# Transposing keys and probabilities on VectorE with a block diagonal query, and splitting the last load, in a one-core decode kernel

## The chip, the cores and the metric

The kernel runs on one core of a Trainium2 chip. The metric is the device time of one execution in microseconds (us). All times below are of undisturbed ("fast") runs; the runs of the two kernels compared agree within 0.5 us. A profiled execution also gives a span, from the first to the last instruction, which is about 1.8 us shorter than the time. Times inside a profile count from the start of that span.

## The reference, cut to what matters

One token (x of 1024 elements) is decoded. Part A is attention over a cache of 65,536 keys and values, with 32 query heads in 4 groups of 8 that share keys and values, each of 128 dimensions. Part B is a gated MLP. A gate mixes both.

```python
q = (x @ wq)                                   # 1024 x 4096
scores = einsum('bhqd,bhkd->bhqk', q, k) * Dh ** (-0.5)
p = softmax(scores)
o = einsum('bhqk,bhkd->bhqd', p, v)
a = o.reshape(...) @ wo                        # 4096 x 1024
z = gelu(x @ w_in)                             # 1024 x 3584
b = (z1 * (w_sp * layernorm(z2) + b_sp)) @ w_out
out = g * a + (1 - g) * b                      # g = sigmoid(sum(x * gate_w))
```

In bf16 the cache and the weights are 162 MB, all read once. There is little arithmetic per byte.

## The kernel before

All large inputs come through one ring of five slots, about 4 MB each, loaded by one queue in a fixed order: wq, then keys with w_in and w_out in between, then pairs of key units and value units in turn, at last wo. A load into a slot is issued when the slot's old content has been used. A unit is 8192 keys (or values) of one group, 2 MB.

The key path before: TensorE transposes 128x128 blocks of fp32 (each fp32 is two bf16 features), VectorE and ScalarE copy them from PSUM, and 32-row matmuls make the scores.

```python
def k_piece(n, j):                       # four of these for a unit
    sl, key = use(("k", n))
    for b in (2 * j, 2 * j + 1):
        def tr(e, b=b, pb=pb):
            for t in range(4):
                ins = e.transpose(pf(pb)[:, 128 * t:128 * (t + 1)],
                                  sl[:, 128 * (4 * b + t):128 * (4 * b + t + 1)], idf)
            return ins
        P("PE", tr, r=["idf", key], w=[B(pb)])
        if b in (2, 5, 7):
            P("ACT", lambda e, ...: e.activation(ktb(i), pbf(pb), ACTF.Copy), ...)
        else:
            P("DVE", lambda e, ...: e.tensor_copy(ktb(i), pbf(pb)), ...)
    # ... cut: s_piece() multiplies with the padded query, 8 matmuls for half a unit
```

The ring, and the end of the kernel:

```python
def done(key):                           # frees the slot of a load, issues the next load into it
    n = place[key][0]
    if key == stream[n][0][-1]:
        issue(n + NS + 1)
# ... cut
for i in range(4):                       # wo in four loads of 2 MB; 32 matmuls for each
    sl, key = use(("wo", i))
    # ... cut: 8 rows c times 4 column groups q, accumulated in one bank
P("DVE", lambda e: e.tensor_tensor(orow[0:97, :], pf(FB)[0:97, 0:QW], brow[0:97, :], ALU.add), ...)
# then the store of the output
```

## Time and profile before

| | before |
|---|---|
| time, median | 390.6 us |
| span of the profile | 389.0 us |
| loaded from HBM | 162.0 MB |
| last load seen as landed | 384.5 us |

The page of the kernel before cuts the span into 40 slices of 9.7 us. Digits are tenths of busy time; PEclk is the clock granted to TensorE, in tenths; DMA is the mean busy share of the 16 DMA engines, and the last row is what they moved.

```profile
...
PE   0000689988997998696888696968686949665423
...
DVE  3000181626756675353645353547453526410110
...
PEclk9999996775999999696989696989896969955685
DMA  8999999999999999999999999999999999999991
GB/s 324 431 431 438 415 397 445 440 432 426 431 426 426 424 426 438 430 431 424 430 431 430 431 426 431 430 431 430 433 431 430 429 430 431 430 431 423 428 414 83
...
```

DMA is busy in every slice but the first and the last, at about 430 GB/s. The other rows have gaps everywhere, so the loads set the pace: 162.4 MB at 431 GB/s are 377 of the 389 us.

The DMA queues of the same page (packets, MB, share of 16 engines' time): q1 brings the loads. q8 and q14 fetch instructions.

```profile
...
q1 hardware_dynamic: 5912, 162.01, 97.3%
q8 instruction: 21, 0.34, 0.4%
...
q14 instruction: 4, 0.03, 0.0%
...
```

The chain that ended last, by engine, and the costliest groups (busy us, mean ns of one, then the idle time ahead of them and what ended it):

```profile
...
DMA 62%; PE 33%; DVE 3%; ACT 1%; issue 1%; ACTq 0%; DVEq 0%
...
```

```profile
...
L440 PE MATMUL pb<-arena 128*128 128x128 f32 x1024 | 155.5, 304 | 39.5 <-DMA arena<-in_A_k_cache_dram 38.9
...
L448 DVE COPY arena<-pb 128x1024 bf16<-128x1024 bf16 x160 | 107.4, 687 | 117.1 <-PE pb L440 115.2
L445 ACT ACTIVATE arena<-pb 128x1024 bf16<-128x1024 bf16 x96 | 97.9, 1020 | 162.1 <-PE pb L440 162.1
L510 PE MATMUL pb<-arena 128*32 128x512 bf16 x512 | 39.0, 432 | 15.9 <-DMA arena<-in_A_v_cache_dram 11.7
L464 PE MATMUL pb<-arena 128*32 128x512 bf16 x512 | 45.1, 431 | 3.6 <-ACT arena L445 1.9
...
```

L440 is the key transposes, L448 and L445 their copies, L464 the scores and L510 the product of probabilities and values. The transposes are the largest thing on TensorE, 155.5 us, but the idle time ahead of them ends with a load of keys.

The end, from the timeline in order of time (start, duration, instruction):

```profile
...
374.68 1.04 PE L653 MATMUL pb<-arena 128*1 128x256 bf16 x32 [2.06 <-DMA arena<-in_A_wo_dram]
...
384.54 1.88 PE L653 MATMUL pb<-arena 128*1 128x256 bf16 x32 [3.08 <-DMA arena<-in_A_wo_dram]
386.47 0.43 DVE L659 TENSOR_TENSOR arena<-pb,arena 97x256 bf16<-97x256 f32 x1 [14.06 <-PE pb L653]
386.92 0.63 SPq L662 DMA_DIRECT2D out_dram<-arena  x1
```

The last quarter of wo is seen to have landed at 384.54, then come 32 matmuls, one add and the store. The same 32 matmuls took 1.04 us at 374.68, where the granted clock was 1.00, and 1.88 us at 384.54, where it was 0.50. In between TensorE had been idle for 3.86 us, had run the 32 matmuls before them in 1.88 us (379.59, clock 0.50), and had been idle again for 3.08 us.

### The profile page before, as it was taken

Reading aid. Unit: us, or ns where it says so; the run is one execution under the profiler, and the core shown is the slowest. Engines: PE = TensorE matmul, PEld = TensorE weight load, DVE = VectorE, ACT = ScalarE, POOL = GpSimd, SP = SyncE. Lnnn points to the kernel's source line nnn. Section 1 sums busy time; section 2 is a strip of 40 time slices with the busy share of each in tenths; the row PEclk is TensorE's granted clock in tenths of the full one; section 3 lists DMA queues with packets and bytes.
Section 4 is the critical chain, followed back from the end, with each engine's and each line's share of the span. In section 5 each row is a group of like instructions: output and inputs, shape, how many; then the busy total and the mean of one; then the engine's idle time right before and its main releaser. Section 6 shows DMA issues by size and latency. Waiting matters only on the chain.

```text
span 389.0 us, 6080 instructions
## 1 busy us (share of the span) xinstructions
PE 267.3 (69%) x2692; PEld 181.6 (47%) x2692; DVE 159.7 (41%) x354; ACT 124.3 (32%) x171; POOL 1.5 (0%) x8
## 2 busy tenths in 40 slices
PE   0000689988997998696888696968686949665423
PEld 0000269786776665454555454545455536221111
DVE  3000181626756675353645353547453526410110
ACT  1000041423556656161435161615251606231000
POOL 1000000000000000000000000000000000000000
PEclk9999996775999999696989696989896969955685
DMA  8999999999999999999999999999999999999991
GB/s 324 431 431 438 415 397 445 440 432 426 431 426 426 424 426 438 430 431 424 430 431 430 431 426 431 430 431 430 433 431 430 429 430 431 430 431 423 428 414 83
DMA packets 6769, 162.39 MB, mean 418 GB/s; under 512 B 1492, under 2 KB 1496, under 8 KB 1496
## 3 DMA queue, kind: packets, MB, share of 16 engines
q1 hardware_dynamic: 5912, 162.01, 97.3%
q8 instruction: 21, 0.34, 0.4%
q10 hardware_dynamic: 832, 0.00, 0.1%
q14 instruction: 4, 0.03, 0.0%
HBM read 162.01 MB, written 0.00 MB: 417 GB/s over the span
## 4 chain that ended last, share of the span: by engine, by line
DMA 62%; PE 33%; DVE 3%; ACT 1%; issue 1%; ACTq 0%; DVEq 0%
DMA arena<-in_A_k_cache_dram 38%; PE pb L440 18%; DMA arena<-in_gate_w_dram 10%; DMA arena<-in_A_v_cache_dram 8%; DMA arena<-in_A_wo_dram 6%; PE pb L464 5%; PE pb L557 3%; PE pb L510 3%; PE pb L396 1%; DVE arena L448 1%; PE pb L498 1%; ACT arena L445 0%; PE pb L653 0%; PE pb L605 0%; DVE arena L421 0%
## 5 line engine op out<-in xcount | busy, mean ns | idle before, releaser
L440 PE MATMUL pb<-arena 128*128 128x128 f32 x1024 | 155.5, 304 | 39.5 <-DMA arena<-in_A_k_cache_dram 38.9
L440 PEld LDWEIGHTS pb<-arena 128*128 128x128 f32 x1024 | 127.7, 157 | 80.3 <-DMA arena<-in_A_k_cache_dram 42.5
L448 DVE COPY arena<-pb 128x1024 bf16<-128x1024 bf16 x160 | 107.4, 687 | 117.1 <-PE pb L440 115.2
L445 ACT ACTIVATE arena<-pb 128x1024 bf16<-128x1024 bf16 x96 | 97.9, 1020 | 162.1 <-PE pb L440 162.1
L510 PE MATMUL pb<-arena 128*32 128x512 bf16 x512 | 39.0, 432 | 15.9 <-DMA arena<-in_A_v_cache_dram 11.7
L464 PE MATMUL pb<-arena 128*32 128x512 bf16 x512 | 45.1, 431 | 3.6 <-ACT arena L445 1.9
L378 PE MATMUL pb<-arena 128*128 128x1 f32 x2 | 0.6, 363 | 40.8 <-DVE arena L377 40.8
L491 ACT ACTIVATE arena<-arena 128x512 bf16<-128x512 f32 x32 | 22.8, 714 | 15.4 <-PE pb L498 13.5
L510 PEld LDWEIGHTS pb<-arena 128*32 128x32 bf16 x512 | 11.7, 102 | 30.9 <-issue 19.8
L470 DVE TENSOR_SCALAR_CACHE_REDUCE arena<-pb 128x512 f32<-128x512 f32 x32 | 21.9, 686 | 6.4 <-PE pb L464 5.8
L501 DVE COPY arena<-pb 128x512 bf16<-128x512 bf16 x32 | 13.3, 416 | 24.7 <-PE pb L498 24.7
L378 PEld LDWEIGHTS pb<-arena 128*128 128x128 f32 x2 | 0.5, 313 | 40.8 <-DVE arena L377 40.8
L464 PEld LDWEIGHTS pb<-arena 128*32 128x32 bf16 x512 | 8.3, 96 | 16.9 <-issue 8.4
L498 PE MATMUL pb<-arena 128*128 128x128 bf16 x128 | 15.3, 255 | 0.0
L376 DVE TENSOR_TENSOR arena<-arena 128x8 f32<-128x8 bf16 x1 | 0.2, 168 | 36.1 <-DMA arena<-in_gate_w_dram 36.1
L498 PEld LDWEIGHTS pb<-arena 128*128 128x128 bf16 x128 | 11.5, 117 | 5.7 <-issue 4.2
L557 PEld LDWEIGHTS pb<-arena 128*128 128x128 bf16 x224 | 13.7, 159 | 0.0
L557 PE MATMUL pb<-arena 128*128 128x1 bf16 x224 | 13.7, 198 | 0.0
L653 PE MATMUL pb<-arena 128*1 128x256 bf16 x128 | 5.8, 342 | 9.0 <-DMA arena<-in_A_wo_dram 9.0
L380 ACT ACTIVATE arena<-pb 128x1 f32<-128x1 f32 x1 | 0.2, 171 | 37.0 <-PE pb L378 37.0
L653 PEld LDWEIGHTS pb<-arena 128*1 128x1 bf16 x128 | 3.2, 99 | 11.2 <-DMA arena<-in_A_wo_dram 6.5
L659 DVE TENSOR_TENSOR arena<-pb,arena 97x256 bf16<-97x256 f32 x1 | 0.4, 426 | 14.1 <-PE pb L653 14.1
(87 smaller groups left out, 59.8 us busy)
## 6 DMA issues: line engine op xcount, KB each, us to landing
arena<-in_A_k_cache_dram SPq DMA_DIRECT2D x16, 4096.0 KB, 29.9
arena<-in_A_v_cache_dram SPq DMA_DIRECT2D x16, 4096.0 KB, 34.3
arena<-in_A_wq_dram SPq DMA_DIRECT2D x2, 4096.0 KB, 17.2
arena<-in_A_wo_dram SPq DMA_DIRECT2D x4, 2048.0 KB, 30.5
arena<-in_B_w_in_dram SPq DMA_DIRECT2D x2, 3584.0 KB, 27.8
arena<-in_B_w_out_dram SPq DMA_DIRECT2D x1, 3584.0 KB, 20.5
arena<-in_A_x_dram ACTq DMA_DIRECT2D x1, 2.0 KB, 22.3
arena<-in_gate_w_dram ACTq DMA_DIRECT2D x1, 2.0 KB, 39.0
```

Of the source, the lines that this page charges most:

```text
L396: ins = e.matmul(pf(OB)[32 * cg:32 * cg + 2, :], xw[:, 3 * c + 1 - s:3 * c + 3 - s], sl[:, WQ_N * k + 512 * (4 * s + cg):WQ_N * k + 512 * ...
L440: ins = e.transpose(pf(pb)[:, 128 * t:128 * (t + 1)], sl[:, 128 * (4 * b + t):128 * (4 * b + t + 1)], idf)
L445: P("ACT", lambda e, i=i, pb=pb: e.activation(ktb(i), pbf(pb), ACTF.Copy), w=[("kt", i % NKTS), B(pb)])
L448: P("DVE", lambda e, i=i, pb=pb: e.tensor_copy(ktb(i), pbf(pb)), w=[("kt", i % NKTS), B(pb)])
L464: ins = e.matmul(pf(SCB)[32 * cg:32 * (cg + 1), :], qpad[:, v:v + 32], vw(ktb(first + cg), ev, [[2, 512]]), start=(c == 0 and ev == 0), st ...
L470: P("DVE", lambda e: e.tensor_scalar(scs(n), pf(SCB), 0.0, None, op0=ALU.add, op1=ALU.max, accum_out=maxc[:, n:n + 1]), w=[("sc", n % NSC) ...
L491: P("ACT", lambda e: e.activation(psb(n), scs(n), ACTF.Exp, bias=gcol(g, K_NB), scale=SCALE, accum_out=lp[:, n:n + 1]), r=[("sc", n % NSC) ...
L498: ins = e.transpose(pbf(PTB)[:, 128 * xi:128 * (xi + 1)], psb(n)[:, 128 * xi:128 * (xi + 1)], idb)
L501: P("DVE", lambda e: e.tensor_copy(ptsb(n), pbf(PTB)[:, 0:512]), w=[("ptsb", n % 2), B(PTB)])
L510: ins = e.matmul(pf(OB)[32 * cg:32 * (cg + 1), :], ptsb(n)[:, 128 * xi + 32 * cg:128 * xi + 32 * (cg + 1)], vw(sl, 128 * (8 * cg + 2 * xi) ...
L557: ins = e.matmul(pf(MB)[:, z:z + 1], vw(sl, c0, [[FC, 128]]), xT[:, 2 * i + k:2 * i + k + 1], start=(i == 0 and k == 0 and z == 0), stop=( ...
L653: ins = e.matmul(pf(FB)[32 * q:32 * q + 1, 0:QW], ovec[:, 8 * i + c:8 * i + c + 1], sl[:, DO * c + QW * q:DO * c + QW * (q + 1)], start=(i ...
```

## The change

Its intent is to take the key transposes and their copies off TensorE, PSUM and ScalarE. VectorE transposes 32x32 blocks from SBUF to SBUF. After such a transpose, each quarter of the partitions holds 32 feature pairs of the keys of that quarter alone, so one matmul over 128 partitions would add up four different keys. The query is therefore laid out block diagonally: rows of the result belong to (quarter, piece, head), and the weights are zero where the quarters differ. Four matmuls, for the even and odd features of two halves, add up the 128 features. The probabilities are transposed in the same way. The maximum becomes one for each head, which saves a correction later. The last quarter of wo is loaded in three parts, so that fewer matmuls follow the last landing.

```diff
-        for b in (2 * j, 2 * j + 1):
-            P("PE", tr, ...)                       # 4 fp32 transposes of 128x128
-            P("ACT" or "DVE", ... copy of the bank ...)
+        P("DVE", lambda e: e.transpose(ktb(i).bitcast(F32), sl[:, 2048 * j:2048 * (j + 1)].bitcast(F32)),
+          r=[key], w=[("kt", i % NKTS)])
+        def f(e):
+            for fe in range(4):
+                f2, ev = fe // 2, fe % 2
+                o = QP * fe + 24 - 8 * j
+                ins = e.matmul(pf(sb), qpad[g % 2][:, o:o + 128], vw(ktb(i), 64 * f2 + ev, [[128, 16], [2, 32]]),
+                               start=(j == 0 and fe == 0), stop=(j == 3 and fe == 3))
+            return ins
 ... cut: query layout, one maximum per head
     def pt_piece(n):
-        ... 4 TensorE transposes into PSUM, one copy ...
+        P("DVE", lambda e: e.transpose(ptsb(n), psb(n)), r=[("psb", n % 2)], w=[("ptsb", n % 2)])
 ... cut: 16 matmuls for values as before, other order of blocks
-    for i in range(4):
-        load([("wo", i)], [(0, rows(A_wo, i, 8))])
+    WO = [(0, 0, 8), (1, 0, 8), (2, 0, 8), (3, 0, 4), (3, 4, 6), (3, 6, 8)]
+    for i, c0, c1 in WO:
+        load([("wo", i, c0)], [(0, rows(A_wo, i, 8)[:, DO * c0:DO * c1])])
```

More of the change, by code (lines that the diff above doesn't have):

```diff
@@ L168, in bass_gated_mix__gqa_block_cached__mixer_gmlp__decode_kernel @@
     SLOT = 16384
-    NB = TILES // 8
-    NKTS = 7
+    QP = 152
+    NKTS = 3
     NSC = 10
@@ L187, in bass_gated_mix__gqa_block_cached__mixer_gmlp__decode_kernel @@
     for name, n in [
-        ("RING", NS * SLOT), ("KT", NKTS * 1024), ("SC", NSC * 1024), ("PSB", 1024), ("PTSB", 1024),
-        ("QPAD", G * 128), ("IDB", 128), ("IDF", 256), ("BM", 256), ("ONES", 256), ("SEL", 16 * 32),
+        ("RING", NS * SLOT), ("KT", NKTS * 2048), ("SC", NSC * 1024), ("PSB", 1024), ("PTSB", 1024),
+        ("QPAD", 2 * 4 * QP), ("IDB", 128), ("IDF", 256), ("BM", 256), ("ONES", 256), ("SEL", 16 * 32),
         ("M16", 32), ("M8", 16), ("M32", 64), ("MQ", 32), ("OT", 256), ("XT", KC), ("GW", KC), ("WB", 2), ("MAXC", 2 * G * NU), ("LP", 2 * G * NU),
-        ("COLS", 2 * 64), ("DM", 32), ("QT", 32), ("XW", 3 * KC), ("SELE", 256), ("OSC", 512), ("OV", OC), ("Z", 2 * 28), ("Z2", 2 * 28),
+        ("COLS", 2 * 64), ("DM", 32), ("QT", 32), ("QALL", 128), ("XW", 3 * KC), ("OSC", 512), ("OV", OC), ("Z", 2 * 28), ("Z2", 2 * 28),
         ("ZG", 2 * 28), ("ZE", 2 * 28), ("YB", FC), ("BROW", 2 * QW), ("OROW", QW),
@@ L212, in bass_gated_mix__gqa_block_cached__mixer_gmlp__decode_kernel @@
     xT, gw, wb = ab("XT", KC), ab("GW", KC), ab("WB", 2)
-    qpad = ab("QPAD", G * 128)
+    qpad = [ab("QPAD", 4 * QP, 4 * QP * i) for i in range(2)]
+    qall = ab("QALL", 128)
     maxc, lp, colt = af("MAXC", G * NU), af("LP", G * NU), af("COLS", 64)
@@ L224, in gcol @@
         return col(C_G4 + 11 * g + i)
-    (K_M, K_NB, K_MH, K_D, K_W, K_L, K_LW, K_RL, K_F) = range(9)
+    (K_M, K_NB, K_MH, K_L, K_RL, K_F) = range(6)
     def slot(n):
         return ab("RING", SLOT, (n % NS) * SLOT)
-    ktb = lambda i: ab("KT", 1024, (i % NKTS) * 1024)
+    ktb = lambda i: ab("KT", 2048, (i % NKTS) * 2048)
     scs = lambda n: af("SC", 512, (n % NSC) * 512)
@@ L236, in bass_gated_mix__gqa_block_cached__mixer_gmlp__decode_kernel @@
     bank = [nc.alloc_psum_tensor("pb%d" % i, [128, 512], F32) for i in range(8)]
-    KTB = [0, 1, 2, 3]
-    SCB, PTB, OB, MB = 4, 5, 6, 7
+    FB, PTB, OB, MB = 0, 5, 6, 7
+    SCB = [3, 4]
     pf = lambda i: bank[i][:, :]
@@ L252, in bass_gated_mix__gqa_block_cached__mixer_gmlp__decode_kernel @@
     P("POOL", lambda e: e.tensor_copy(idb, idf), r=["idf"], w=["idb"])
-    P("POOL", lambda e: e.memset(qpad, 0.0), w=["qpad"])
+    for i in range(2):
+        P("POOL", lambda e, i=i: e.memset(qpad[i], 0.0), w=[("qpad", i)])
     P("DVE", lambda e: e.memset(ones, 1.0), w=["ones"])
@@ L257, in bass_gated_mix__gqa_block_cached__mixer_gmlp__decode_kernel @@
     P("DVE", lambda e: e.memset(pf(OB), 0.0), w=[B(OB)])
+    P("DVE", lambda e: e.memset(pf(FB), 0.0), w=[B(FB)])
     P("DVE", lambda e: e.memset(xw, 0.0), w=["xw"])
@@ L369, in bass_gated_mix__gqa_block_cached__mixer_gmlp__decode_kernel @@
     P("DVE", lambda e: e.tensor_reduce(mq, vw(idf, 0, [[1, 16], [16, 8]]), AXX, ALU.add), r=["idf"], w=["mq"])
-    for ev in range(2):
-        P("DVE", lambda e, ev=ev: e.tensor_copy(vw(ab("SELE", 128, 128 * ev), 0, [[64, 2], [1, 64]]),
-                                                vw(idb, ev, [[0, 2], [2, 64]])), r=["idb"], w=["sele"])
+    sele = ab("SC", 512, (NSC - 1) * 1024)
+    KSE = ("sc", NSC - 1)
+    for fe in range(4):
+        P("DVE", lambda e, fe=fe: e.tensor_copy(vw(sele, 128 * fe, [[32, 4], [1, 32]]),
+                                                vw(idb, 64 * (fe // 2) + fe % 2, [[0, 4], [2, 32]])),
+          r=["idb"], w=[KSE])
     P("DVE", lambda e: e.tensor_tensor(z2[:, 0:KC], xT, gw, ALU.mult), r=["xT", "gw"], w=["z2"])
@@ L414, in f @@
     def f(e):
-        for ev in range(2):
-            ins = e.matmul(pf(PTB)[:, 32 * ev:32 * (ev + 1)], ab("SELE", 128, 128 * ev), qT, start=True, stop=True)
-        return ins
-    P("PE", f, r=["sele", "qT"], w=[B(PTB)])
-    for g in range(G):
-        for par in range(2):
-            P("DVE", lambda e, g=g, par=par: e.tensor_copy(
-                vw(qpad, 128 * g + 8 * par, [[80, 2], [32, 2], [1, 8]], 64 * par, 64),
-                vw(pf(PTB), 8 * g, [[0, 2], [32, 2], [1, 8]], 64 * par, 64)), r=[B(PTB)], w=["qpad"])
+        for fe in range(4):
+            ins = e.matmul(pf(PTB)[:, 32 * fe:32 * (fe + 1)], sele[:, 128 * fe:128 * (fe + 1)], qT, start=True, stop=True)
@@ L426, in bass_gated_mix__gqa_block_cached__mixer_gmlp__decode_kernel, with q_piece @@
+        return ins
+    P("PE", f, r=[KSE, "qT"], w=[B(PTB)])
+    P("DVE", lambda e: e.tensor_copy(qall, pf(PTB)[:, 0:128]), w=["qall", B(PTB)])
     nbatch = [0]
     pend = []
+    def q_piece(g):
+        for pb in range(4):
+            P("DVE", lambda e, pb=pb: e.tensor_copy(vw(qpad[g % 2], 24 + 32 * pb, [[QP, 4], [1, 8]], 32 * pb, 32),
+                                                    vw(qall, 8 * g, [[32, 4], [1, 8]], 32 * pb, 32)),
+              r=["qall"], w=[("qpad", g % 2)])
     def k_piece(n, j):
+        g, u = KV[n]
+        if u == 0 and j == 0:
+            q_piece(g)
@@ L431, in k_piece @@
         sl, key = use(("k", n))
-        sl = sl.bitcast(F32)
-        for b in (2 * j, 2 * j + 1):
-            i = nbatch[0]
-            nbatch[0] += 1
-            pb = KTB[i % 4]
-            def tr(e, b=b, pb=pb):
-                for t in range(4):
-                    ins = e.transpose(pf(pb)[:, 128 * t:128 * (t + 1)],
-                                      sl[:, 128 * (4 * b + t):128 * (4 * b + t + 1)], idf)
-                return ins
-            P("PE", tr, r=["idf", key], w=[B(pb)])
-            if b in (2, 5, 7):
-                P("ACT", lambda e, i=i, pb=pb: e.activation(ktb(i), pbf(pb), ACTF.Copy),
-                  w=[("kt", i % NKTS), B(pb)])
-            else:
-                P("DVE", lambda e, i=i, pb=pb: e.tensor_copy(ktb(i), pbf(pb)), w=[("kt", i % NKTS), B(pb)])
+        i = nbatch[0]
@@ new lines, in k_piece @@
+        nbatch[0] += 1
+        P("DVE", lambda e: e.transpose(ktb(i).bitcast(F32), sl[:, 2048 * j:2048 * (j + 1)].bitcast(F32)),
+          r=[key], w=[("kt", i % NKTS)])
+        sb = SCB[n % 2]
+        def f(e):
+            for fe in range(4):
+                f2, ev = fe // 2, fe % 2
[3 more added lines that the diff above has]
+            return ins
@@ L449, in k_piece @@
+        P("PE", f, r=[("qpad", g % 2), ("kt", i % NKTS)], w=[B(sb)])
+        if pend:
+            score_piece(pend.pop(0))
         if j == 3:
             done(("k", n))
-        if j % 2 == 1:
-            pend.append((n, j // 2, nbatch[0] - 4))
-    def s_piece():
-        if not pend:
-            return
-        n, c, first = pend.pop(0)
-        g, u = KV[n]
-        def f(e):
-            for ev in range(2):
-                for cg in range(4):
-                    v = 128 * g + 32 * (2 * c + ev)
-                    ins = e.matmul(pf(SCB)[32 * cg:32 * (cg + 1), :], qpad[:, v:v + 32],
-                                   vw(ktb(first + cg), ev, [[2, 512]]), start=(c == 0 and ev == 0),
-                                   stop=(c == 1 and ev == 1), tile_position=(0, 32 * cg), skip_group_check=True)
-            return ins
-        P("PE", f, r=["qpad"] + [("kt", (first + i) % NKTS) for i in range(4)], w=[B(SCB)])
-        if c == 1:
-            P("DVE", lambda e: e.tensor_scalar(scs(n), pf(SCB), 0.0, None, op0=ALU.add, op1=ALU.max,
-                                               accum_out=maxc[:, n:n + 1]), w=[("sc", n % NSC), ("mx", n), B(SCB)])
-            if u == NU - 1:
-                max_piece(g)
@@ L475, in max_piece, with score_piece @@
+            pend.append(n)
+    def score_piece(n):
+        g, u = KV[n]
+        sb = SCB[n % 2]
+        P("DVE", lambda e: e.tensor_scalar(scs(n), pf(sb), 0.0, None, op0=ALU.add, op1=ALU.max,
+                                           accum_out=maxc[:, n:n + 1]), w=[("sc", n % NSC), ("mx", n), B(sb)])
+        if u == NU - 1:
+            max_piece(g)
     def max_piece(g):
@@ L477, in max_piece @@
           r=[("mx", NU * g + u) for u in range(NU)], w=[("m", g)])
-        P("DVE", lambda e: e.tensor_scalar(gcol(g, K_NB), gcol(g, K_M), -SCALE, None, op0=ALU.mult),
-          r=[("m", g)], w=[("nb", g)])
-    def weight_piece(g):
         P("DVE", lambda e: e.tensor_scalar(dm, m16, gcol(g, K_M), None, op0=ALU.mult), r=["m16", ("m", g)], w=["dm"])
@@ L484, in weight_piece @@
         P("DVE", lambda e: e.tensor_reduce(gcol(g, K_MH), pf(MB)[:, 0:16], AXX, ALU.max), w=[("mh", g), B(MB)])
-        P("DVE", lambda e: e.tensor_tensor(gcol(g, K_D), gcol(g, K_M), gcol(g, K_MH), ALU.subtract),
-          r=[("m", g), ("mh", g)], w=[("d", g)])
-        P("ACT", lambda e: e.activation(gcol(g, K_W), gcol(g, K_D), ACTF.Exp, scale=SCALE), r=[("d", g)], w=[("w", g)])
+        P("DVE", lambda e: e.tensor_scalar(gcol(g, K_NB), gcol(g, K_MH), -SCALE, None, op0=ALU.mult),
+          r=[("mh", g)], w=[("nb", g)])
     def exp_piece(n):
@@ L495, in pt_piece @@
     def pt_piece(n):
-        def f(e):
-            for xi in range(4):
-                ins = e.transpose(pbf(PTB)[:, 128 * xi:128 * (xi + 1)], psb(n)[:, 128 * xi:128 * (xi + 1)], idb)
-            return ins
-        P("PE", f, r=["idb", ("psb", n % 2)], w=[B(PTB)])
-        P("DVE", lambda e: e.tensor_copy(ptsb(n), pbf(PTB)[:, 0:512]), w=[("ptsb", n % 2), B(PTB)])
+        P("DVE", lambda e: e.transpose(ptsb(n), psb(n)), r=[("psb", n % 2)], w=[("ptsb", n % 2)])
     def pv_piece(n):
@@ L507, in f @@
         def f(e):
-            for xi in range(4):
-                for cg in range(4):
-                    ins = e.matmul(pf(OB)[32 * cg:32 * (cg + 1), :],
-                                   ptsb(n)[:, 128 * xi + 32 * cg:128 * xi + 32 * (cg + 1)],
-                                   vw(sl, 128 * (8 * cg + 2 * xi), [[4096, 2], [1, 256]]),
-                                   start=(u == 0 and xi == 0), stop=(u == NU - 1 and xi == 3),
-                                   tile_position=(0, 32 * cg), skip_group_check=True)
+            for b in range(16):
+                cg = b % 4
+                ins = e.matmul(pf(OB)[32 * cg:32 * (cg + 1), :], ptsb(n)[:, 32 * b:32 * (b + 1)],
+                               vw(sl, 128 * b, [[2048, 4], [1, 128]]), start=(u == 0 and b < 4),
+                               stop=(u == NU - 1 and b >= 12), tile_position=(0, 32 * cg), skip_group_check=True)
             return ins
@@ L523, in out_piece @@
           r=[("lp", NU * g + u) for u in range(NU)], w=[("l", g)])
-        P("DVE", lambda e: e.tensor_tensor(gcol(g, K_LW), gcol(g, K_L), gcol(g, K_W), ALU.mult),
-          r=[("l", g), ("w", g)], w=[("lw", g)])
-        P("PE", lambda e: e.matmul(pf(MB)[:, 0:1], bm, gcol(g, K_LW), start=True, stop=True),
-          r=["bm", ("lw", g)], w=[B(MB)])
+        P("PE", lambda e: e.matmul(pf(MB)[:, 0:1], bm, gcol(g, K_L), start=True, stop=True),
+          r=["bm", ("l", g)], w=[B(MB)])
         P("DVE", lambda e: e.reciprocal(gcol(g, K_RL), pf(MB)[:, 0:1]), w=[("rl", g), B(MB)])
-        P("DVE", lambda e: e.scalar_tensor_tensor(gcol(g, K_F), gcol(g, K_RL), gcol(g, K_W), col(C_G),
-                                                  op0=ALU.mult, op1=ALU.mult),
-          r=[("rl", g), ("w", g), "g"], w=[("f", g)])
+        P("DVE", lambda e: e.tensor_scalar(gcol(g, K_F), gcol(g, K_RL), col(C_G), None, op0=ALU.mult),
+          r=[("rl", g), "g"], w=[("f", g)])
         P("DVE", lambda e: e.tensor_scalar(osc, pf(OB), gcol(g, K_F), None, op0=ALU.mult),
@@ L625, in bass_gated_mix__gqa_block_cached__mixer_gmlp__decode_kernel @@
         if k is None and pend:
-            s_piece()
+            score_piece(pend.pop(0))
         if v is not None and v not in started:
@@ L630, in bass_gated_mix__gqa_block_cached__mixer_gmlp__decode_kernel @@
             if k is not None:
-                ready = len(pend)
                 k_piece(k, j)
-                s_piece() if ready else None
             if j == 1 and v is not None:
                 pt_piece(v)
-            if j == 2 and nxt is not None and (k is not None or not pend):
+            if j == 2 and nxt is not None:
                 start_exp(nxt)
@@ L639, in bass_gated_mix__gqa_block_cached__mixer_gmlp__decode_kernel, with f @@
                 pv_piece(v)
-        if v is not None and v % NU == 0:
-            weight_piece(v // NU)
         for a in aux:
             (win_piece if a[0] == "win" else wout_piece)(a[1])
-    FB = KTB[0]
-    for i in range(4):
-        sl, key = use(("wo", i))
-        def f(e, i=i, sl=sl):
-            for c in range(8):
+    for i, c0, c1 in WO:
+        sl, key = use(("wo", i, c0))
+        def f(e, i=i, sl=sl, c0=c0, c1=c1):
+            for c in range(c0, c1):
                 for q in range(4):
+                    o = DO * (c - c0) + QW * q
                     ins = e.matmul(pf(FB)[32 * q:32 * q + 1, 0:QW], ovec[:, 8 * i + c:8 * i + c + 1],
-                                   sl[:, DO * c + QW * q:DO * c + QW * (q + 1)],
-                                   start=(i == 0 and c == 0), stop=(i == 3 and c == 7), tile_position=(0, 32 * q),
-                                   skip_group_check=True)
+                                   sl[:, o:o + QW], start=(i == 0 and c == 0), stop=(i == 3 and c == 7),
+                                   tile_position=(0, 32 * q), skip_group_check=True)
             return ins
         P("PE", f, r=[("ovec", i), key], w=[B(FB)])
+        done(("wo", i, c0))
     P("DVE", lambda e: e.tensor_tensor(orow[0:97, :], pf(FB)[0:97, 0:QW], brow[0:97, :], ALU.add),
```

## The prediction

> **What bounds the kernel now.** The loads. The page's row of slices shows DMA busy at 0.9 or more in every slice but the first and last, mostly at 424 to 431 GB/s; queue q1 is busy for 97.3% of the span. 162.4 MB at 431 GB/s is 377 us of a 389.0 us span; the rest is the start and the end. TensorE's 69% (key transposes 155.5 us), VectorE's 41% and ScalarE's 32% lie under the loads. In the chain of waits DMA has 62%; TensorE's part lies in the first 135 us (it starts late, since gate_w lands at 40 us), yet windows there average 428 GB/s: five ring slots of 4 MB hide it.
>
> The end, from the timeline: the last quarter of wo lands at 384.54, then 32 matmuls at half clock (1.9 us), one add (0.43 us), the store (about 2 us). The load rate falls off from 376 to 384, as the DMA engines do not finish together; this stays.
>
> **What the change does.**
> - Removes 1024 fp32 TensorE transposes (155.5 us busy), their 256 evictions (VectorE 107.4 us, ScalarE 97.9 us), 128 transposes of probabilities (15.3 us) and their copies (13.3 us).
> - Adds 128 VectorE transposes of 128x1024 fp32.[...] The trace's 512-column fp32 evictions took 0.69 us[...]. 128 x 1.2 = 155 us, 32 probability transposes of 0.6 us (estimate, 19 us) and the score reductions (22 us): VectorE rises to about 205 us, 53%. ScalarE falls to about 27 us.
> - Scores become 512 full-width matmuls of 512 columns[...]. TensorE falls to roughly 170 to 200 us.
> - Splits the last load, so that 8 matmuls instead of 32 follow the last bytes: 1.9 us becomes 0.5.
>
> **Critical path.** A pair of key units and one of value units take 19.5 us to load. VectorE needs for them 8 x 1.2 + 2 x 0.7 + 2 x 0.6 = 12.2 us: it keeps up. In the key-only stage two units need about 11 us of VectorE and win 6.7 us of TensorE; I find each slot free 7 us or more before the queue would run dry. So the loads stay the limit. Gained: 1.4 us from the split, and 0.3 us as the instruction fetch (0.34 MB) shrinks by about 40%. 390.6 - 1.7 = 388.9 us.
>
> **Predicted: 388.9 us, range 387.3 to 391.3.** Chances: over 2% faster 0.03, within 2% 0.91, slower 0.06.
>
> **What would show it.** Right: DMA share 0.9 or more in all middle slices at about 430 GB/s; VectorE transposes near 1.2 us; more TensorE idle put down to k_cache and v_cache loads; 8 matmuls (0.5 us) between the last landing and the add; last landing within 1 us of 384.5. Wrong: dips of GB/s between 60 and 135 us, or the load queue waiting on transposes or score matmuls.
>
> **What would make it wrong.** [...]VectorE becomes the limit and the time goes to 392 to 400.[...]

Five passages of this text are cut, since no trace or run of this case shows what they rest on: two on how the 1.2 us for a key transpose was arrived at; the time of the score matmuls; the condition for VectorE to become the limit (key transposes at about twice the cost); and a sum for TensorE at half clock. TensorE's 170 to 200 us contains a term, 110 us for the score matmuls. The 1.2 and 0.6 us for VectorE's transposes, and with them 155, 19, 205, 12.2 and 11 us, were my estimates, which no trace showed at that time; the changed kernel's shows 1.216 and 0.679 us.

## The result, and the profile after

The changed kernel takes 387.72 us (387.70 to 387.94) against 390.62 us: 2.9 us less. The ratio is 0.9926, with a 95% interval of 0.9909 to 0.9943. It is the mean time of one kernel's fast runs over that of the other's in the same rounds, so it is not quite the ratio of the medians.

The slices of the changed kernel, 9.6 us each:

```profile
...
PE   0000668983886888472688383827883929543354
...
DVE  4000078335999997574597574735984748511010
...
PEclk9999969695899999696789697956697978866555
DMA  8999999999999999999999999999999999999994
GB/s 326 435 435 442 374 442 426 429 436 433 435 408 419 435 435 430 428 435 427 431 431 435 433 435 431 435 423 429 435 431 426 428 432 435 430 431 428 419 419 190
...
```

The load rate has hardly changed (420 GB/s in the mean of the span, 418 before). VectorE is now the busiest engine in slices 11 to 15 (96 to 145 us), and TensorE has more gaps. The span is 385.9 us (389.0 before).

Its queues:

```profile
...
q1 hardware_dynamic: 6200, 162.01, 98.1%
q8 instruction: 12, 0.20, 0.2%
...
q14 instruction: 4, 0.03, 0.0%
...
```

The loads are the same 162.01 MB. The instruction fetches of q8 have gone from 21 packets to 12, because 1150 matmuls with their weight loads are gone (2692 became 1542; with 1128 put back as padding, below, the fetches are 21 again).

Its chain by engine, and its groups:

```profile
...
DMA 53%; PE 22%; DVE 22%; issue 1%; ACT 0%; ACTq 0%; DVEq 0%
...
```

```profile
...
L457 PE MATMUL pb<-arena 128*128 128x512 bf16 x512 | 154.4, 442 | 78.5 <-DVE arena L449 76.2
L449 DVE STREAM_TRANSPOSE arena<-arena 128x1024 f32<-128x1024 f32 x128 | 151.3, 1216 | 56.7 <-DMA arena<-in_A_k_cache_dram 50.5
...
L487 ACT ACTIVATE arena<-arena 128x512 bf16<-128x512 f32 x32 | 23.0, 720 | 208.5 <-DVE arena L492 155.3
L492 DVE STREAM_TRANSPOSE arena<-arena 128x512 bf16<-128x512 bf16 x32 | 21.7, 679 | 18.3 <-PE pb L501 18.3
L470 DVE TENSOR_SCALAR_CACHE_REDUCE arena<-pb 128x512 f32<-128x512 f32 x32 | 21.7, 678 | 5.7 <-PE pb L457 5.5
...
```

L449 is the new key transpose: 1216 ns for 1024 fp32 elements per partition. L492 transposes the probabilities, L457 makes the scores, and L487 is the exponential that was there before. The rest of ScalarE's work is gone.

Its end:

```profile
...
382.76 0.60 PE L635 MATMUL pb<-arena 128*1 128x256 bf16 x8 [0.65 <-DMA arena<-in_A_wo_dram]
383.41 0.42 DVE L641 TENSOR_TENSOR arena<-pb,arena 97x256 bf16<-97x256 f32 x1 [13.41 <-PE pb L635]
383.86 0.62 SPq L644 DMA_DIRECT2D out_dram<-arena  x1
```

The last landing is at 382.76 instead of 384.54, and 8 matmuls follow it instead of 32. So the traces show two gains: the loads end 1.7 to 1.8 us earlier, and the tail behind them is 1.3 us shorter (the last matmuls take 0.60 us instead of 1.88). The prediction had the second and only 0.3 us of the first.

To see why the loads end earlier, one more record of the trace is needed. In the trace every large load has 16 semaphore increments at different times, and the kernel goes on at the last of them: for the last load of the kernel before they come from 379.13 to 384.41 us, and the matmuls start at 384.54. The page counts 16 DMA engines; I read each increment as one of them being done with its part. The records do not name the engine, so "engine" below stands for this reading. The table, worked out from these increments, gives for some loads of the kernel before the first landing (us) and how much later each of the sixteen came, in order:

```
load   first   the sixteen, us after the first
  4    51.16   0.00 0.11 0.12 0.15 0.16 0.18 0.20 0.21 0.22 0.27 0.28 0.30 0.31 0.33 0.61 0.65
  5    59.71   0.00 0.11 0.14 0.16 0.17 0.19 0.20 0.23 0.24 0.26 0.28 0.29 0.31 0.32 0.59 2.17
 14   145.90   0.00 0.14 0.17 0.20 0.22 0.59 0.91 1.25 1.70 1.71 1.73 1.81 1.83 1.84 1.86 2.20
 15   155.60   0.00 0.15 0.17 0.22 0.23 0.60 0.92 1.26 1.71 1.71 1.72 1.82 1.86 1.86 1.87 3.71
 29   291.57   0.00 0.13 0.17 0.19 0.22 0.61 0.92 2.22 3.25 3.26 3.33 3.36 3.38 3.39 3.40 3.73
 30   301.29   0.00 0.13 0.17 0.19 0.21 0.60 0.92 2.23 3.24 3.25 3.33 3.36 3.37 3.39 3.40 5.27
 40   379.13   0.00 0.12 0.16 0.18 0.19 0.59 0.90 3.18 3.34 3.35 3.35 4.76 4.77 4.86 4.88 5.27
```

From load 4 to load 5 one engine falls behind by about 1.5 us and never makes it up. The others follow one after the other; by load 14 half of them are behind. Then one falls behind a second time (15), and a third time (30). q8's packets, 16,384 bytes each, start at 58.9 us (the first), 156.1 us (the ninth) and 299.7 us (the seventeenth): just where the last engine steps back, and every eighth. Compared load by load, each of q8's 21 fetches is followed by one landing that moves back by about 1.5 us (1.4 to 1.8), and each of q14's four, 8,192 bytes each, by one that moves back by 0.6 to 1.1 us. That a fetch holds up the one engine that carries it is likewise a reading of this pattern, called theory F below.

- Theory F: each instruction fetch sets one DMA engine back by about 1.5 us, in turn. The loads wait for the engine that was set back most. The changed kernel has fewer instructions, so its loads end earlier.
- Rival S: the split of the last load evens out its end.
- Rival T: something else in the new arrangement (transposes on VectorE, other times at which slots come free) does it.

A second suspicion, theory Q, came from the loads' issue times. In the changed kernel load 11 is issued at 105.14, only 1.95 us before load 10, the only one still under way, begins to land. From load 10 to load 11 the spread (last minus first of the sixteen) grew by 1.0 us, and most engines, not one, fell behind. There the queue seems to have run nearly dry. The prediction had claimed 7 us or more everywhere.

### The profile page after: what moved, and what is told of

The parts are those of the page before. It is cut to its first block, busy times and chain, and to the rows that moved or that the text cites. A ratio compares the mean times of both kernels' runs of the same rounds, so it can differ in the third digit from the quotient of the medians.

```text
span 385.9 us, 3595 instructions
## 1 busy us (share of the span) xinstructions
PE 227.0 (59%) x1542; PEld 84.7 (22%) x1542; DVE 210.5 (55%) x326; ACT 30.6 (8%) x71; POOL 2.1 (1%) x9
## 3 DMA queue, kind: packets, MB, share of 16 engines
q1 hardware_dynamic: 6200, 162.01, 98.1%
HBM read 162.01 MB, written 0.00 MB: 420 GB/s over the span
## 4 chain that ended last, share of the span: by engine, by line
DMA 53%; PE 22%; DVE 22%; issue 1%; ACT 0%; ACTq 0%; DVEq 0%
DMA arena<-in_A_k_cache_dram 31%; DVE arena L449 16%; PE pb L457 13%; DMA arena<-in_gate_w_dram 10%; DMA arena<-in_A_v_cache_dram 9%; PE pb L543 3%; DMA arena<-in_A_wo_dram 3%; PE pb L501 2%; DVE arena L470 2%; PE pb L404 2%; DVE arena L492 1%; PE pb L635 1%; DVE arena L518 0%; DVE arena L438 0%; PE pb L523 0%
## 5 line engine op out<-in xcount | busy, mean ns | idle before, releaser
L457 PE MATMUL pb<-arena 128*128 128x512 bf16 x512 | 154.4, 442 | 78.5 <-DVE arena L449 76.2
L449 DVE STREAM_TRANSPOSE arena<-arena 128x1024 f32<-128x1024 f32 x128 | 151.3, 1216 | 56.7 <-DMA arena<-in_A_k_cache_dram 50.5
L457 PEld LDWEIGHTS pb<-arena 128*128 128x128 bf16 x512 | 45.4, 106 | 181.9 <-DVE arena L449 128.1
L501 PE MATMUL pb<-arena 128*32 128x512 bf16 x512 | 39.3, 442 | 20.3 <-DMA arena<-in_A_v_cache_dram 17.8
L487 ACT ACTIVATE arena<-arena 128x512 bf16<-128x512 f32 x32 | 23.0, 720 | 208.5 <-DVE arena L492 155.3
L492 DVE STREAM_TRANSPOSE arena<-arena 128x512 bf16<-128x512 bf16 x32 | 21.7, 679 | 18.3 <-PE pb L501 18.3
L501 PEld LDWEIGHTS pb<-arena 128*32 128x32 bf16 x512 | 12.9, 107 | 44.5 <-issue 36.5
L543 PEld LDWEIGHTS pb<-arena 128*128 128x128 bf16 x224 | 13.8, 161 | 0.4
L386 PEld LDWEIGHTS pb<-arena 128*128 128x128 f32 x2 | 0.5, 314 | 40.6 <-DVE arena L385 40.6
L404 PE MATMUL pb<-arena 128*2 128x512 bf16 x64 | 6.4, 584 | 0.9 <-DVE arena L395 0.9
L487 ACT ACTIVATION_READ_ACCUMULATOR arena<-arena 128x1 f32 x32 | 6.0, 186 | 0.0
L635 PEld LDWEIGHTS pb<-arena 128*1 128x1 bf16 x128 | 3.4, 109 | 10.5 <-DMA arena<-in_A_wo_dram 7.6
L523 PE MATMUL pb<-arena 128*128 128x128 bf16 x16 | 1.8, 243 | 5.2 <-DVE arena L518 5.2
```

The source lines that it names most:

```text
L386: P("PE", lambda e: e.matmul(pf(PTB)[:, 0:1], ones, col(C_GS), start=True, stop=True), r=["ones", "gs"], w=[B(PTB)])
L404: ins = e.matmul(pf(OB)[32 * cg:32 * cg + 2, :], xw[:, 3 * c + 1 - s:3 * c + 3 - s], sl[:, WQ_N * k + 512 * (4 * s + cg):WQ_N * k + 512 * ...
L449: P("DVE", lambda e: e.transpose(ktb(i).bitcast(F32), sl[:, 2048 * j:2048 * (j + 1)].bitcast(F32)), r=[key], w=[("kt", i % NKTS)])
L457: ins = e.matmul(pf(sb), qpad[g % 2][:, o:o + 128], vw(ktb(i), 64 * f2 + ev, [[128, 16], [2, 32]]), start=(j == 0 and fe == 0), stop=(j == ...
L487: P("ACT", lambda e: e.activation(psb(n), scs(n), ACTF.Exp, bias=gcol(g, K_NB), scale=SCALE, accum_out=lp[:, n:n + 1]), r=[("sc", n % NSC) ...
L492: P("DVE", lambda e: e.transpose(ptsb(n), psb(n)), r=[("psb", n % 2)], w=[("ptsb", n % 2)])
```

## The experiments

Each kernel ran in five rounds (the doubled transposes in three) beside the kernel before, which had 390.57 to 390.73 us. All results were correct against the reference.

### One part alone: the split

```diff
 kernel before, and:
-    for i in range(4):
-        load([("wo", i)], [(0, rows(A_wo, i, 8))])
+    WO = [(0, 0, 8), (1, 0, 8), (2, 0, 8), (3, 0, 4), (3, 4, 6), (3, 6, 8)]
+    ... loads and matmuls as in the changed kernel
```

> The kernel before with only the last load split. Theory F (the landings at the end are late because the DMA engines also fetch TensorE's instructions): as many instructions as before, so the last landing stays near 384.4 us and the sixteen completions of the last load stay 5.2 us apart; only the 24 matmuls less after the last landing count, 1.3 us: 389.3 us. Rival S (the split itself evens out the end of the loads): last landing near 382.8, 387.7 us.

Measured: 389.28 us (ratio 0.9965, 0.9951 to 0.9978). There were 21 fetches on q8, the last landing was at 384.25 and the spread 4.88 us. Theory F named 384.4, 5.2 and 389.3. Rival S falls: the split does not move the last landing, it shortens what follows it, by 1.3 us.

### The other part alone: no split

```diff
 changed kernel, and:
-    WO = [(0, 0, 8), (1, 0, 8), (2, 0, 8), (3, 0, 4), (3, 4, 6), (3, 6, 8)]
+    WO = [(0, 0, 8), (1, 0, 8), (2, 0, 8), (3, 0, 8)]
```

> The changed kernel with the last load whole again. Theory F: the instruction stream stays short, so the last landing is near 382.5 us with a spread near 3.2 us, then 32 matmuls at half clock (1.9 us): 388.9 us. Rival S: the last landing goes back to about 384.4 us and the time to 390.5 us.

Measured: 389.27 us (0.9966, 0.9952 to 0.9980), the last landing at 382.47, the spread 3.29, 12 fetches on q8. So the part with the transposes gives 1.3 us too, all ahead of the last landing. (The profiled execution was the fastest of the five, 388.82 us, so its landing is 1.9 us earlier than before, while the median run gains 1.3.) Rival S falls a second time. This run cannot tell F from T.

### Instructions put back as padding, first try

Here the changed kernel gets back about as many TensorE instructions as it lost, as matmuls of one column that nobody reads.

```diff
+    def pad(n):
+        def f(e):
+            for _ in range(n):
+                ins = e.matmul(pf(1)[0:1, 0:1], idb[:, 0:1], idb[:, 0:1], start=True, stop=True)
+            return ins
+        P("PE", f, r=["idb"], w=[B(1)])
+    pad(512)                       # ahead of the product with wq
...
                 k_piece(k, j)
+                if k >= 10:
+                    pad(7)
```

> The changed kernel with 1128 one-column matmuls that do nothing (2256 TensorE instructions with their weight loads), 512 of them in TensorE's idle time before 40 us, 616 spread over the later key pieces; loads unchanged. Theory F: about 21 instruction fetches instead of 12, completions of one load already 1.5 us or more apart before 45 us (0.3 to 0.5 without the padding), about 5 us apart at the end, last landing near 384.5 us, 389.4 us. Rival (the transposes' place or the loads' order set the spread): spread 3.2 us, 387.7 us, as the changed kernel.

Measured: 401.96 us, 12 us longer than expected. The experiment was built wrongly. Its slices:

```profile
...
DMA  8999908999998999999999999999999999999994
GB/s 351 433 423 420 411 15 318 424 436 438 421 419 374 444 442 418 421 449 431 424 429 428 444 426 421 433 441 430 423 428 434 433 428 426 433 434 433 416 420 170
...
```

And its chain, in order of time (start, duration, what):

```profile
...
1.21 38.87 DMA arena<-in_gate_w_dram
41.19 5.59 PE pb L399 x221
...
49.31 3.34 PE pb L399 x128
...
58.06 5.08 PE pb L412 x59
...
```

The first 512 matmuls stood behind the one that waits for gate_w until 40 us, and TensorE ran them in the program's order: at 41 to 58 us, ahead of the product with wq (L412), which frees the first slots. The load that is issued at 45.76 in the changed kernel was issued at 61.43; the queue was empty, and one slice moved 15 GB/s. The run says nothing for or against F, but it shows what a slot costs that comes free 16 us late. It also shows that the delays did not last through this empty queue: behind that stall the spread was 0.93 us, ahead of it 1.47 us. I read this as engines that were behind catching up while the others had nothing to do.

### Padding, second try

The same, with the first 512 matmuls moved ahead of the matmul that waits for gate_w, into idle time.

```diff
+    pad(512)
     P("PE", lambda e: e.matmul(pf(PTB)[:, 0:1], ones, col(C_GS), start=True, stop=True), ...)
```

> The padding again, now with its first 512 matmuls ahead of the first matmul that waits for gate_w, so that it lies in TensorE's idle time and delays no load (in the first try it stood behind that wait and held the ring up for 12 us). Theory F: about 21 fetches, several before 40 us, completions of one load some 1.5 us apart or more by 30 us, 5 us apart at the end, last landing near 384.5 us, 389.4 us. Rival: spread 3.2 us at the end, 387.7 us.

Measured: 389.01 us (388.90 to 389.72; ratio 0.9962, 0.9948 to 0.9976). The last landing was at 384.49, the spread 5.16 us. The queues:

```profile
...
q8 instruction: 21, 0.34, 0.3%
...
q14 instruction: 4, 0.03, 0.0%
...
```

The fetches are 21 again, the first at 7.5 us, and the first load of all already lands with one engine 1.68 us behind (0.30 in the changed kernel). By 34 us four engines were more than 1.4 us behind, while no fetch had come in the changed kernel by then. The loads and the VectorE transposes are those of the changed kernel, and yet the last landing is that of the kernel before. This is theory F as expected; rival T falls as the explanation of the 1.3 us. (The profiled execution was one of the two slower ones, 389.46 us. By the medians the padding gives back 1.3 of the 1.6 us that lie between the split alone and the changed kernel.) TensorE did have more work here, which the next run takes away.

### Padding on an engine that nothing waits for

```diff
 changed kernel, and:
+    for _ in range(1152):
+        P("POOL", lambda e: e.memset(ab("SCR", 2), 0.0), r=["scr"], w=["scr"])
```

> The changed kernel with 1152 tiny memsets on GpSimd, each after a wait for the one before, so some 2300 instructions more on an engine that nothing waits for; TensorE and the loads are unchanged. If any engine's instruction fetch puts a DMA engine back (theory F, wide form): the extra 147 KB come as some 18 fetches of 8 KB, completions of one load 4.5 to 6 us apart at the end, 389 to 390.5 us. If only TensorE's stream counts, or its matmuls rather than its bytes: spread 3.2 us, 387.7 us.

Measured: 390.32 us (0.9989, 0.9976 to 1.0001), the last landing at 384.93, the spread 4.60 us. The engines' line and the queues:

```profile
...
PE 226.1 (58%) x1542; PEld 84.1 (22%) x1542; DVE 210.6 (54%) x326; ACT 30.6 (8%) x71; POOL 116.7 (30%) x1161
...
q8 instruction: 12, 0.20, 0.2%
...
q14 instruction: 13, 0.11, 0.1%
...
```

TensorE has its 1542 matmuls and 12 fetches on q8, but q14 has gone from 4 packets of 8 KB to 13 (9 more and not the 18 expected: 74 KB are 64 bytes for each of the 1152 memsets, as the 147 KB of the 9 fetches that the change saves on q8 are for 2300 instructions, so I read that their waits took no instructions of their own), and the last landing is 2.2 us later. So it is the instruction stream, of GpSimd here as of TensorE in the run before, and not TensorE's work. Not all of the 2.2 us is spread: the first of the sixteen landed 0.8 us later than in the changed kernel too. The trace shows where that began. gate_w landed at 40.94 us instead of 40.11, the loads behind it were issued some 0.85 us later, and load 11 was issued at 106.02, only 1.0 us before load 10 began to land; load 10 still came in time (107.05, 107.09 in the changed kernel), load 11 no longer (117.75 instead of 116.93). That is the nearly dry queue of theory Q. The other 1.45 us are spread, and they look different from q8's pattern: five times, after q14's fetches at 72.9, 93.2, 133.4, 153.5 and 173.6 us, the largest delay grew by 0.6 to 0.7 us (the memsets ran on evenly all that time, so the steps belong to the fetches), and at the end one landing was 4.60 us behind and the other fifteen within 2.49. So q14's fetches seem to have hit the same engine again and again instead of taking turns.

### The wait at 105 us taken away

The mixer of part B is a serial chain of small operations between VectorE, ScalarE and TensorE; in the changed kernel both big engines do only its small steps from 88 to 94 us. Here it is cut into stages between the key pieces.

```diff
     def mixer_piece():
         ...
         P("ACT", lambda e: e.activation(ze, z2, ACTF.Exp, scale=GELU_K), ...)
+        yield                      # likewise after two matmuls and the square root
...
                 k_piece(k, j)
+                if mixing and next(mixing[0], True):
+                    mixing.clear()
```

> The changed kernel with the mixer's short serial chain cut in five stages between the key pieces, so that TensorE and VectorE do not stand still for it; the work is the same. Theory Q (in the changed kernel the queue ran nearly dry at 105 us, a load issued only 2 us before the load ahead of it began to land, which cost the slow engines 1 us): that load is issued 5 us or more ahead, the spread stays near 1.9 us until the second round of fetches, last landing near 381.9 us, 386.8 us. Rival (the step of the spread at 110 to 120 us is an instruction fetch): no change, 387.7 us.

Measured: 387.70 us, no change. Half of theory Q held: load 11 was issued 4.25 us ahead instead of 1.95, and its spread was 1.69 us instead of 2.95, so the step there was the nearly dry queue. But this did not reach the end: at load 29, after the ninth fetch at 291.5 us, the spread rose from 2.1 to 3.1 us, and at the end it was 3.08 (3.15 in the changed kernel). In the changed kernel the same fetch raised it by 0.16 us only. The landings tell why. In both kernels this fetch moved one engine from about 1.5 us behind the first to about 3 (1.44 to 2.97 us in the changed kernel, about 1.5 to 3.09 in the staged one). In the changed kernel another engine had been 2.81 us behind since the wait at 105 us, so the fetch added only 0.16 to the largest delay; and the largest delay counts, not the sum. A wait that was really removed was worth nothing.

### The transposes at twice their cost

```diff
+        P("DVE", lambda e: e.transpose(ktb(i).bitcast(F32), sl[:, 2048 * j:2048 * (j + 1)].bitcast(F32)),
+          r=[key, ("kt", i % NKTS)], w=[("kt", i % NKTS)])     # once more into the same buffer
```

> Each key piece is transposed twice into the same buffer[...]. My estimate from this case's durations: a key unit then takes VectorE 8 x 1.17 + 0.68 us and a value unit 0.68, 10.7 us against 9.7 us of loading, so VectorE sets the pace from about 51 us on and the time comes to 405 to 420 us, with dips of the load rate below 420 GB/s in many slices. Rival (VectorE would still be hidden by the ring): under 392 us.

Measured: 470.59 us (1.2058), far over both what I expected here and what the prediction gave for key transposes at about twice the cost (392 to 400). Three rows of its slices, and windows (us; busy us of PE, PEld, DVE, ACT, POOL; clock; DMA share; GB/s):

```profile
...
DVE  3000898919999899999995999999969999997530
...
DMA  8999998797087926999796687997968869988995
GB/s 356 412 429 418 422 387 355 320 402 317 0 359 310 409 76 283 402 397 426 303 425 269 294 359 314 430 404 320 413 275 359 348 258 425 404 362 359 423 426 231
...
```

```profile
...
51.00:151.00 100.00, 66.92 (x412) 28.99 (x412) 86.44 (x104) 3.38 (x5) 0.00 (x0) 0.66 0.76 314
151.00:428.00 277.00, 173.62 (x750) 46.55 (x750) 261.16 (x294) 19.45 (x48) 0.00 (x0) 0.73 0.83 345
428.00:468.00 40.00, 22.48 (x306) 9.08 (x306) 12.19 (x29) 6.30 (x16) 0.00 (x0) 0.72 0.87 367
...
```

VectorE is the limit, as foreseen, and the load rate falls to 314 and 345 GB/s. Both estimates divided VectorE's work by the steady pace alone. The windows show what they left out. The first eight key units took the 100 us of the first window, 12.5 us each (VectorE needs about 10.5 for one: four times 1.214 + 1.246, and 0.653 for the score reduction), since VectorE stood idle there, for 8.3 us in one piece until the product with w_in was done, and had the mixer's small steps to do. The other 24 took 277 us, 11.5 us each, with VectorE 94% busy. Then 40 us follow for the last values and for wo, whose loads could no longer run ahead. The same kernel with single transposes is far from this: VectorE is busy for 64.50 us of the window from 200 to 300.

### Fewer instructions, and a version that beats both

In the staged kernel, x becomes the weight in the product with w_in and w_in streams 512 columns at a time; rows are turned back by 8 small matmuls. This makes 72 matmuls of 224.

```diff
-                for z in range(2 * FC):
-                    ins = e.matmul(pf(MB)[:, z:z + 1], vw(sl, c0, [[FC, 128]]), xT[:, 2 * i + k:2 * i + k + 1], ...)
+                for h in range(2):
+                    for cg in range(4):
+                        ins = e.matmul(pf(1 + h)[32 * cg:32 * cg + 1, 0:128 * nc_], xT[:, 2 * i + k:2 * i + k + 1],
+                                       vw(sl, F * k + FH * h + 4 * cg, [[1, nc_], [FC, 128]]), ...)
```

> The staged kernel with the product of x and w_in turned round: x is the weight and w_in streams 512 columns at a time, 72 matmuls in place of 224, 304 TensorE instructions less. Theory F: 11 fetches instead of 12; the ninth, which starts the second round and sets the last engine, comes some 40 us later (about 330 us) but still before the end, so the last landing moves little: 387.5 us, within 0.4 us of the changed kernel. Rival (bytes fetched count evenly, 1.2 us for 9 fetches): 0.15 us. A second rival (TensorE's instructions do not matter, earlier freed slots do): no change at all, since none of the slots is late.

Measured: 387.62 us; 11 fetches on q8, the last landing at 382.64, the spread 3.39. The time is that of the changed kernel within the scatter. The saved fetch did not lower the largest delay; by their sizes both F and its even-count rival were expected within 0.4 us, so this run decides nothing between them. One step came otherwise than expected: the largest delay rose from 2.32 to 3.29 us at load 31, after q14's fetch at 309.2 us, before q8's ninth at 331.7.

```diff
 the same, and:
-    WO = [..., (3, 4, 6), (3, 6, 8)]
+    WO = [..., (3, 4, 6), (3, 6, 7), (3, 7, 8)]
```

> The same with the last load split once more, so that 4 matmuls instead of 8 follow the last landing: 0.3 us less at half clock, 387.2 us. If the 2 KB packets of the last two loads cost more than that, no gain.

Measured: 387.48 us (387.35 to 387.57; 0.9919, 0.9906 to 0.9933), 0.14 us less than without the finer tail, where 0.3 us was expected. To compare on one chip, the changed kernel and this one ran once more:

> The changed kernel itself, beside the others of this call: 387.7 us again, spread near 3.2 us.

> The best version so far again, on the same chip as the changed kernel: 387.5 us, 0.2 us under it.

Measured: 387.70 us and 387.40 us (0.9924 and 0.9917). The version with all three edits is 0.3 us faster. It is the fastest seen, but the intervals of the ratios overlap, so a small gain is likely rather than shown.

### All together

| kernel | fetches q8, q14 | first / last landing of the last load, us | spread, us | time, us |
|---|---|---|---|---|
| before | 21, 4 | 379.13 / 384.41 | 5.27 | 390.6 |
| split only | 21, 4 | 379.37 / 384.25 | 4.88 | 389.28 |
| no split | 12, 4 | 379.18 / 382.47 | 3.29 | 389.27 |
| changed kernel | 12, 4 | 379.56 / 382.72 | 3.15 | 387.7 |
| padding on TensorE, second try | 21, 4 | 379.33 / 384.49 | 5.16 | 389.01 |
| padding on GpSimd | 12, 13 | 380.33 / 384.93 | 4.60 | 390.32 |
| staged mixer | 12, 4 | 379.38 / 382.46 | 3.08 | 387.70 |
| fewer, with finer tail | 11, 4 | 379.34 / 382.62 | 3.28 | 387.48 |

The times are medians; landings and spreads are of the profiled execution, which was not the median one everywhere (388.82 us without the split, 389.46 with the second padding, 389.92 with that on GpSimd, 387.42 staged). The first landing hardly moves in seven of the eight kernels, the last one moves with the fetches, and the time moves with the last landing and the tail behind it.

## Why the prediction was right or wrong

The time, 387.7 us, lies in the stated range, 0.4 us from its lower end; the sign and the class were right. Of the 2.9 us gained it had named 1.7; that the time still lies in the range is owed to the range's width and not to the mechanism.

- "The loads stay the limit": right. The DMA row of the slices is unchanged, 162.01 MB on q1 in both.
- VectorE's cost: right. 1.2 us for a key transpose (128x1024 in fp32) was measured as 1.216; it was my estimate, and the kernel before had no such transpose to show it. The bf16 transposes (128x512) took 0.679 us instead of 0.6, so 512 elements more per partition, in the other type, went with 537 ns more. VectorE came to 210.5 us (about 205 predicted).
- The split: right. 1.4 us were predicted; the split alone gave 1.3.
- "0.3 us as the instruction fetch shrinks": the step that was mis-sized. The prediction spread the bytes evenly, 0.14 MB at 431 GB/s. As the landings are read above, each of q8's fetches set one DMA engine back by about 1.5 us (the largest delay of the kernel before went from 0.65 to 2.17, from 2.20 to 3.71 and from 3.73 to 5.27 us), and the kernel went on only at the last of a load's sixteen landings. The part without the split gave 1.3 us, and putting the instructions back took the last landing from 382.72 to 384.49. "The DMA engines do not finish together; this stays" was wrong for the same reason: the spread went from 5.27 to 3.15 us. So the last landing, named as a sign of a right prediction if within 1 us of 384.5, came at 382.76.
- "Each slot free 7 us or more before the queue would run dry": wrong for four loads. Counted as for load 11 above, loads 5, 7, 11 and 12 were issued 5.4, 6.4, 1.95 and 3.8 us ahead. For load 11 the cause was the standstill in the mixer, which I had not added up with the pieces around it; the rate fell to 408 GB/s in slice 12 (106 to 116 us). It cost nothing in the end, as the staged kernel shows.
- TensorE at 170 to 200 us: it was 227 us. The score matmuls took 442 ns in the mean (154.4 us in all instead of the 110). A piece of four took 1.04 us in the median where the granted clock was full (89 of 128 pieces) and 1.89 us where it was half (25 pieces). The 110 us were my estimate and too low even at the full clock: there the trace has a matmul of 512 columns start every 217 ns, and the last one then takes 378 ns to its end. It does not matter for the time.
- Doubled transposes: "392 to 400 us" was wrong by 70 us, for the reasons shown by the windows.

What the large removal itself is worth: the second padding restores the instruction count and keeps VectorE's transposes and the split; it takes 389.01 us (388.90 to 389.72), where the split alone takes 389.28; beside the kernel before the ratios are 0.9962 and 0.9965. So these runs show no gain of moving 155 us of transposes between engines beyond that scatter. The gain came from the shorter instruction stream and the shorter tail. The transposes of the probabilities were not tried by themselves.

## What to carry to other kernels

When loads bound a kernel, as here, do not expect work that is moved off an engine to gain its busy time (155 us moved off TensorE: 389.01 us, against 389.28 without the move); ask what it does to the loads' queue, and count instructions too: here 9 fetches more on q8 (second padding) went with a last landing at 384.49 us instead of 382.72, and the kernel used a load only at the last of its sixteen landings. Look at the spread of the sixteen landings of a load over the run, not at the mean share of DMA time, and split the last load so that little work follows it. A delay counts only if it falls on what is already last: taking away the wait at 105 us was worth nothing (387.70 us, as the changed kernel), since another engine was as far behind at the end (3.08 us, 3.15 with the wait). With doubled transposes a key unit took 12.5 us in the first stage against 11.5 us later, so an engine with spare time in the steady stage may have none in the first.
